# Retention, routed experts and an MLP in one kernel: buffers, the place of the bias and of the counts, and the order of loads at two seams

## The chip, the core and the metric

The kernel runs on one core of a Trainium2 chip as one launch. The metric is the device time of one execution in microseconds (us); the kernel before takes 1440.12 us in the median of three runs (1436.64 to 1443.65). In what follows PE is the matrix engine (PEld its weight loads), DVE, ACT and POOL are the vector, scalar and GpSimd engines, SP is the engine that issues most of the DMAs; SPq and ACTq are the queues of SP and ACT.

## The reference

Three steps, each on the output of the one before. Inputs are q, k, v of 8 sequences, 8 heads, 576 positions and 64 per head; then a mixture of 8 experts over 4608 tokens of 512 numbers; then an MLP of width 2048.

```python
# 1. retention: no softmax, a decay per head
gamma = 1.0 - 2.0 ** (-5.0 - np.arange(H))
Dmat = np.where(rel >= 0, gamma[:, None, None] ** rel, 0.0)       # rel = i - j
attn = np.matmul(q @ k.T / sqrt(64) * Dmat, v)
x = attn.transpose(0, 2, 1, 3).reshape(4608, 512)
# 2. each token goes to the expert with the largest logit
logits = x @ w_gate + modality_bias[modality_id]
e_idx = np.argmax(logits, axis=1)
gate_w = softmax(logits)[arange(N), e_idx]
out[mask] = gate_w[mask, None] * (relu(x[mask] @ w1[e]) @ w2[e])  # mask = e_idx == e
# 3.
h = out @ w_in
y = (h - tanh(h)) @ w_out
```

## The kernel before

**Retention, in tiles.** `for t in range(NTILE)` runs over 36 tiles of 128 tokens; nine tiles are two sequences. SP loads three arrays for a tile: qk, vk (`load_tile`) and, for the first nine, the decay factors gx (`load_gx`). They are loaded `AHEAD` = 4 tiles ahead. On PE a tile is the scores of the *next* tile (`scores(t+1)`, L305), and then `attend(t)`: the inter part, from the state of the tokens before (L341), the intra part, from the masked scores a and the scaled values vs (L349), and the update of the state (L364). DVE masks the scores (L309) and multiplies the result by gx into xt (L374). ACT copies the state (L368). POOL makes vs, the values times a decay, in `scaled` (L315), two tiles ahead and into two buffers. Inter comes ahead of intra, but for tiles without an inter part, the tile in which a sequence begins in its middle, and the last tile of all:

```python
after = not inter or mid_t or t == NTILE - 1
```

**Routing, in groups of four tiles.** `route_a`, `route_b` and `route_c` (L405 to L457) make logits, the expert of each token, its slot and its gate. The logits get `bias`, which five POOL operations make ahead of the loop from the modality ids (`mid`) and the two rows of bias (`mb`). `scatter` (L460, L461) has POOL write 128 token numbers into the list of their experts, slot_d, by an indirect DMA. `turn_x` turns a tile on PE (L472), `save_x` scales it by the gate on ACT into xo (L477; two buffers) and stores it to x_d (L478, on ACT's queue).

**The seam to the experts.** An expert's tokens are worked on in units of 400. `choose` (L380) counts after 28 of the 36 tiles and picks an expert that already has 400 tokens. Two tiles later SP loads their numbers (`load_ids`, L154) and POOL gathers the rows with four indirect DMAs (`gather_rows`, L158); PE turns them (`turn_rows`, L148), ACT and DVE split them into a high and a low part (xh L149, xl L150). So unit 0 begins while the routing of the last tiles is open; that is spread over its steps f = 0, 1, 2 (`rest_a`, `rest_b`, `rest_c`). `rest_c` turns the last four tiles on PE, counts (L567) and calls `table`, a chain of small DVE operations that writes which expert, slots and rows every further unit has (utab). `swap` then opens the buffers of the later stages, and issues those weight loads of unit 1 that had been put off (`pend`).

**Units.** A unit has 8 steps f, in each of which PE does 12 matmuls hp (L634) and 12 matmuls acc (L828 to L830); `load_raw` (L696) loads weights, `split_w` splits them on ACT (L703) and DVE (L704). `prep(u, f)` puts the work for the next unit into the steps: for unit 0 the ids of unit 1 at f = 2, their gather at f = 3, the turning of its four blocks of rows (`tr_x`) at f = 5, 6 and 7.

**MLP.** Nine blocks of 512 tokens, hp (L634) and acc (L902 to L904) again; its first matrix is kept in winh and winl, its second is prepared in DRAM during the units (wo_d).

The order on each engine is the order in which this code is written; a framework puts in the waits for buffers and data. A pool with n buffers of a name makes the (n+1)th user wait for the first to be done.

Of the kernel before, what the change touches and what calls it, by code (L numbers as in the profile page):

```python
# [21 lines left out]
DM = H * D  # L22
# [5 lines left out]
AHEAD = 4  # L28
# [73 lines left out]
def kernel(tc, A, out):  # L102
    nc = tc.nc
    with ExitStack() as ctx:
# [12 lines left out]
        wres = pool("wres", 1)  # L117

        ident = keep.tile([128, 128], F32, name="ident")
        winh = wres.tile([128, F3, DM], F32R, name="winh")  # L120
        winl = wres.tile([128, F3, DM], F32R, name="winl")

# [81 lines left out]
        with tc.manual_schedule():  # L204
# [9 lines left out]
            xo_p = p1r("xo", 2, side="right")  # L214
# [49 lines left out]
            load_gx(2)  # L264

# [46 lines left out]
            def scaled(t):  # L312
                qk, vk = gt[t]
                vs = tmp.tile([128, H, D], F32, name="vs")
# [7 lines left out]
            def attend(t):  # L322
# [7 lines left out]
                after = not inter or mid_t or t == NTILE - 1  # L330
# [149 lines left out]
            def store_x(t, spare=False):  # L480
# [7 lines left out]
            bt = xo_p.tile([128, DM], F32, name="xo")  # L488
            midf, midn = bt[:, 0:NTILE], bt[:, NTILE:2 * NTILE]
            b1 = bt[:, 2 * NTILE:(2 + E) * NTILE].rearrange("p (t e) -> p t e", e=E)  # L490
            nc.gpsimd.tensor_copy(out=midf, in_=mid[:, :, 0])
            nc.gpsimd.tensor_scalar(out=midn, in0=midf, scalar1=-1.0, scalar2=1.0, op0=ALU.mult, op1=ALU.add)
            sh = [128, NTILE, E]
            nc.gpsimd.tensor_tensor(out=bias, in0=midn.unsqueeze(2).to_broadcast(sh),
                                    in1=mb[:, 0:1, :].to_broadcast(sh), op=ALU.mult)
            nc.gpsimd.tensor_tensor(out=b1, in0=midf.unsqueeze(2).to_broadcast(sh),
                                    in1=mb[:, 1:2, :].to_broadcast(sh), op=ALU.mult)
            nc.gpsimd.tensor_tensor(out=bias, in0=bias, in1=b1, op=ALU.add)
# [5 lines left out]
            for t in range(NTILE):  # L504
# [5 lines left out]
                if t + 2 < NTILE:  # L510
                    scaled(t + 2)
                if t + AHEAD < NTILE:
                    load_tile(t + AHEAD)
                if t + 3 < PERIOD:
                    load_gx(t + 3)
# [47 lines left out]
            def rest_c():  # L563
                late.extend(range(g * RG, NTILE))
                late_x(RG)
                cp = ps_m.tile([128, E], F32, name="m")
                nc.tensor.matmul(out=cp, lhsT=ones, rhs=cum[:, NRG], start=True, stop=True)  # L567
                table(cp)

# [47 lines left out]
            c1.close()  # L617

# [45 lines left out]
            with ExitStack() as c2:  # L664
# [84 lines left out]
                def swap():  # L749
# [17 lines left out]
                    while pend:  # L767
                        load_raw(pend.pop(0))

                def prep(u, f):  # L770
# [10 lines left out]
                    if u + 1 < UMIN:  # L781
# [4 lines left out]
                        for s in {5: (0,), 6: (1, 2), 7: (3,)}.get(f, ()) if u == 0 else range(f - F1 + SE + 1, f - F1 + SE + 2):  # L786
                            if 0 <= s < SE:
                                tr_x(u + 1, s)
# [170 lines left out]
```

## Time and profile before

| | |
|---|---|
| median of three runs | 1440.12 us (1436.64 to 1443.65) |
| profiled execution | 1445.13 us, of which 1443.4 us are the span of the trace |
| PE busy | 1399.0 us, 97% |
| DVE, ACT, POOL busy | 1044.4, 683.5 and 221.1 us |

Times in the rows are counted from the span's start. Retention and routing fill the stretch up to some 160 us, unit 0 begins at 176 us, unit 1 at about 211, and the MLP fills the second half. In a row of a timeline, the bracket at the end is how long the engine stood idle just before and what ended that.

### The profile page before, as it was taken

To read this page: it belongs to the slowest core of one execution; us is meant where nothing else is said; L and a number is where in the kernel's file an instruction comes from. 1 tells how busy PE (TensorE), PEld (TensorE's weight loads), DVE (VectorE), ACT (ScalarE), POOL (GpSimd) and SP (SyncE) were. 2 spreads that over 40 slices of the span, in tenths; PEclk is the share of its full clock that TensorE was granted. 3 is DMA by queue.
4 is the path that set the end of the run, shared out by engine and by line. 5 is a ranking of instruction groups with operands and counts; after the bars stand their busy time and mean duration, and the time that the engine had idled before them with its cause. 6 is when DMAs were issued, how large, how long until landed. Compare 5 with 4: busy or idle time off the path is not lost.

```text
span 1443.4 us, 22522 instructions
## 1 busy us (share of the span) xinstructions
PE 1399.0 (97%) x8427; PEld 1215.6 (84%) x8427; DVE 1044.4 (72%) x1761; ACT 683.5 (47%) x1269; POOL 221.1 (15%) x288
## 2 busy tenths in 40 slices
PE   6999689999999999989999999999999999999997
PEld 5888589999999999977888888888888888888885
DVE  2666458888888888746777777777777777778764
ACT  0222244444444444444555555555555555565543
POOL 4455421111111111010111101111011110011101
PEclk8999889999999999999999999999999999999999
DMA  9999353454663345516000100001000000000000
GB/s 336 343 333 329 129 185 118 127 132 132 179 189 89 89 90 150 124 33 254 30 30 1 37 23 30 30 9 50 1 30 30 30 30 0 30 30 1 30 1 30
DMA packets 65682, 138.71 MB, mean 96 GB/s; under 512 B 22480, under 2 KB 29328, under 8 KB 65568
## 3 DMA queue, kind: packets, MB, share of 16 engines
q1 hardware_dynamic: 49360, 96.15, 22.1%
q0 software_dynamic: 7904, 21.96, 4.4%
q10 hardware_dynamic: 8304, 19.11, 3.5%
q8 instruction: 68, 1.11, 0.3%
q14 instruction: 46, 0.38, 0.1%
HBM read 135.16 MB, written 39.80 MB: 121 GB/s over the span
## 4 chain that ended last, share of the span: by engine, by line
PE 49%; issue 5%; POOL 0%; DMA 0%; DVE 0%; ACT 0%; POOLq 0%; DVEq 0%; ACTq 0%
PE hp L634 25%; PE acc L902 8%; PE acc L903 8%; PE acc L904 8%; POOL out_dram L927 0%; DMA wout<-wo_d 0%; DVE xh L878 0%; ACT xh L876 0%; DVE xl L885 0%; POOLq L955 0%; DVE xl L887 0%; DVE xl L877 0%; DVE xl L886 0%; POOL nopt L926 0%; DVE lo L881 0%
## 5 line engine op out<-in xcount | busy, mean ns | idle before, releaser
L875 ACT ACTIVATE xh<-hp 128x512 f32<-128x512 f32 x144 | 86.4, 600 | 331.7 <-PE hp L634 313.1
L902 PE MATMUL acc<-wout,hi 128*128 128x512 f32 x576 | 226.0, 392 | 5.2 <-DMA wout<-wo_d 5.2
L634 PE MATMUL hp<-yh,winh 128*128 128x512 f32 x576 | 226.4, 393 | 1.4 <-DVEq L849 1.4
L634 PE MATMUL hp<-yl,winh 128*128 128x512 f32 x576 | 226.2, 393 | 0.0
L634 PE MATMUL hp<-yh,winl 128*128 128x512 f32 x576 | 226.1, 393 | 0.0
L903 PE MATMUL acc<-wout,hi 128*128 128x512 f32 x576 | 225.9, 392 | 0.0
L904 PE MATMUL acc<-wout,lo 128*128 128x512 f32 x576 | 224.9, 390 | 0.0
L877 DVE TENSOR_TENSOR xl<-xh,hp 128x512 f32<-128x512 f32 x144 | 99.1, 688 | 167.8 <-ACT xh L876 167.8
L886 DVE SCALAR_TENSOR_TENSOR xl<-xh,xl 128x512 f32<-128x512 f32 x144 | 128.5, 893 | 15.4 <-DVE xl L885 0.5
L828 PE MATMUL acc<-hi,wh 128*128 128x400 f32 x384 | 137.9, 359 | 0.1
L902 PEld LDWEIGHTS acc<-wout,hi 128*128 128x128 f32 x576 | 108.7, 189 | 29.9 <-ACT xh L875 5.6
L634 PE MATMUL hp<-xl,wh 128*128 128x400 f32 x384 | 133.4, 348 | 0.4 <-DVE xl L150 0.4
L830 PE MATMUL acc<-hi,wl 128*128 128x400 f32 x384 | 133.4, 347 | 0.0
L634 PE MATMUL hp<-xh,wl 128*128 128x400 f32 x384 | 133.2, 347 | 0.0
L634 PE MATMUL hp<-xh,wh 128*128 128x400 f32 x384 | 133.0, 346 | 0.0
L829 PE MATMUL acc<-lo,wh 128*128 128x400 f32 x384 | 132.2, 344 | 0.0
L634 PEld LDWEIGHTS hp<-yh,winh 128*128 128x128 f32 x576 | 108.2, 188 | 25.7 <-PEq L849 1.7
L634 PEld LDWEIGHTS hp<-yh,winl 128*128 128x128 f32 x576 | 108.3, 188 | 24.7
L904 PEld LDWEIGHTS acc<-wout,lo 128*128 128x128 f32 x576 | 108.7, 189 | 23.9 <-DVE lo L881 0.4
L634 PEld LDWEIGHTS hp<-yl,winh 128*128 128x128 f32 x576 | 108.1, 188 | 23.9
L903 PEld LDWEIGHTS acc<-wout,hi 128*128 128x128 f32 x576 | 108.6, 188 | 23.2
L728 ACT ACTIVATE hi<-hp 128x400 fp32r<-128x400 f32 x96 | 48.5, 506 | 166.9 <-PE hp L634 166.9
(162 smaller groups left out, 2526.4 us busy)
## 6 DMA issues: line engine op xcount, KB each, us to landing
raw<-in_w_dram SPq DMA_DIRECT2D x91, 512.0 KB
qk<-in_qk_dram SPq DMA_DIRECT2D x36, 512.0 KB
vk<-in_vk_dram SPq DMA_DIRECT2D x35, 512.0 KB
y_d<-yo SPq DMA_DIRECT2D x12, 800.0 KB
yr<-y_d SPq DMA_DIRECT2D x9, 1024.0 KB
raw<-in_wo_dram SPq DMA_DIRECT2D x16, 512.0 KB
wo_d<-cv_em ACTq DMA_DIRECT2D x16, 512.0 KB
raw<-in_wi_dram SPq DMA_DIRECT2D x16, 512.0 KB
```

The source lines that it names most:

```text
L634: nc.tensor.matmul(out=hp, lhsT=lhs, rhs=rhs, start=j == 0, stop=j == 3 * KD - 1)
L728: nc.scalar.activation(out=hi, in_=hp, func=ACTF.Relu)
L828: nc.tensor.matmul(out=o, lhsT=wh[:, cs], rhs=hi, start=first, stop=False)
L829: nc.tensor.matmul(out=o, lhsT=wh[:, cs], rhs=lo, start=False, stop=False)
L830: nc.tensor.matmul(out=o, lhsT=wl[:, cs], rhs=hi, start=False, stop=last)
L875: nc.scalar.activation(out=u, in_=hp, func=ACTF.Square)
L877: nc.vector.tensor_tensor(out=v, in0=u, in1=hp, op=ALU.mult)
L886: nc.vector.scalar_tensor_tensor(out=v, in0=s, scalar=SQ_C, in1=v, op0=ALU.add, op1=ALU.mult)
L902: nc.tensor.matmul(out=acc[s], lhsT=hi, rhs=wh, start=first, stop=False)
L903: nc.tensor.matmul(out=acc[s], lhsT=hi, rhs=wl, start=False, stop=False)
L904: nc.tensor.matmul(out=acc[s], lhsT=lo, rhs=wh, start=False, stop=last)
```

## The change

Its edits:

- Loads run six tiles ahead (`AHEAD`), for gx as well; the loads of two more tiles stand ahead of the loop.
- vs has four buffers and is made four tiles ahead; xo has four buffers.
- The bias is made after tile 2 (`make_bias`) and not ahead of the loop.
- The last tile has inter ahead of intra, as most tiles have.
- In `rest_c` the count and `table` stand ahead of the last four turns.
- The room of winh and winl is taken when the first pools of the routing are closed, not from the start.
- The weight loads of unit 1 that had been put off are issued in `prep`, behind the ids of unit 1, and not in `swap`.
- Unit 1's blocks of rows are turned two in step 6 and two in step 7 of unit 0, in place of one, two and one in steps 5 to 7.

On POOL, the first vs products of the program and the bias (xo is the scratch tile of the bias), before:

```order
L315 TENSOR_TENSOR vs<-vk,vsc 128x512 x2
L491 CAST xo<-mid 128x36
L492 TENSOR_SCALAR xo<-xo 128x36
L494 TENSOR_TENSOR bias<-xo,mb 128x288
L496 TENSOR_TENSOR xo<-xo,mb 128x288
L498 TENSOR_TENSOR bias<-bias,xo 128x288
L315 TENSOR_TENSOR vs<-vk,vsc 128x512 x8
```

and after:

```order
L314 TENSOR_TENSOR vs<-vk,vsc 128x512 x7
L493 CAST xo<-mid 128x36
L494 TENSOR_SCALAR xo<-xo 128x36
L496 TENSOR_TENSOR bias<-xo,mb 128x288
L498 TENSOR_TENSOR xo<-xo,mb 128x288
L500 TENSOR_TENSOR bias<-bias,xo 128x288
L314 TENSOR_TENSOR vs<-vk,vsc 128x512 x5
```

Five further vs products stand ahead of the bias now: those of tiles 2 to 6.

On POOL, ahead of the gathers of unit 0's rows (L158 before, L154 after; nopt is a small memset that goes with each scatter), before:

```order
L460 MEMSET nopt 128x1
L461 DMA slot_d<-tokid,pos_s 37376x16
L460 MEMSET nopt 128x1
L461 DMA slot_d<-tokid,pos_s 37376x16
L315 TENSOR_TENSOR vs<-vk,vsc 128x512
L460 MEMSET nopt 128x1
L461 DMA slot_d<-tokid,pos_s 37376x16
L460 MEMSET nopt 128x1
L461 DMA slot_d<-tokid,pos_s 37376x16
L315 TENSOR_TENSOR vs<-vk,vsc 128x512
L158 DMA vk<-x_d,idt_74 128x512 x3
L158 DMA vk<-x_d,idt_74 16x512
```

and after:

```order
L314 TENSOR_TENSOR vs<-vk,vsc 128x512
L459 MEMSET nopt 128x1
L460 DMA slot_d<-tokid,pos_s 37376x16
L459 MEMSET nopt 128x1
L460 DMA slot_d<-tokid,pos_s 37376x16
L459 MEMSET nopt 128x1
L460 DMA slot_d<-tokid,pos_s 37376x16
L459 MEMSET nopt 128x1
L460 DMA slot_d<-tokid,pos_s 37376x16
L154 DMA vk<-x_d,idt_69 128x512 x3
L154 DMA vk<-x_d,idt_69 16x512
```

The vs products of the last two tiles stood between and behind the scatters; now the last vs of all is ahead of four scatters in a row.

On SP, behind the last row stores of the routing (x_d<-xg), where the loads for unit 1 begin (utab is the table of units, idt the ids, raw the weights), before:

```order
L679 TENSOR_LOAD utab
L679 ISA x2
L679 TENSOR_LOAD utab
L679 ISA x2
L696 ISA
L696 DMA raw_2516<-in_w_dram 128x1024
L696 ISA
L696 DMA raw_2518<-in_w_dram 128x1024
L679 TENSOR_LOAD utab
L679 ISA x2
L154 ISA
L154 DMA idt<-slot_d 128x4x1
```

and after:

```order
L687 TENSOR_LOAD utab
L687 ISA x2
L150 ISA
L150 DMA idt<-slot_d 128x4x1
L687 TENSOR_LOAD utab
L687 ISA x2
L687 TENSOR_LOAD utab
L687 ISA x2
L704 ISA
L704 DMA raw_2516<-in_w_dram 128x1024
L704 ISA
L704 DMA raw_2518<-in_w_dram 128x1024
```

The ids stood behind two weight loads; now they stand ahead of them.

```diff
--- before.py
+++ after.py
@@ -25,7 +25,7 @@
 TL = 128
 NTILE = NT // TL
 PERIOD = 9
-AHEAD = 4
+AHEAD = 6
 RG = 4
 NRG = NTILE // RG
 UE = 400
@@ -114,12 +114,8 @@
         tok_d = dram.tile([NT + UE, 1], I32, name="tok_d")
         wo_d = dram.tile([F3, 128, 2, DM], F32, name="wo_d")
         keep = pool("keep", 1)
-        wres = pool("wres", 1)
 
         ident = keep.tile([128, 128], F32, name="ident")
-        winh = wres.tile([128, F3, DM], F32R, name="winh")
-        winl = wres.tile([128, F3, DM], F32R, name="winl")
-
         xT_p = [pool("xTa", 1), None]
         idt0 = keep.tile([128, SE], I32, name="idt0")
         pick = keep.tile([1, 2], I32, name="pick")
@@ -211,7 +207,7 @@
             tmp = p1("tmp", 2)
             const = p1r("const", 1, side="right")
             xt_p = p1r("xt", 3, side="right")
-            xo_p = p1r("xo", 2, side="right")
+            xo_p = p1r("xo", 4, side="right")
             sm = p1r("sm", 2, side="right")
             ps_sc = p1("ps_sc", 3, space=PSUM)
             ps_x = p1("ps_x", 1, space=PSUM)
@@ -262,6 +258,9 @@
             nc.scalar.dma_start(out=mb.rearrange("p a e -> p (a e)"), in_=A["mb"].to_broadcast([128, 2 * E]))
             load_tile(3)
             load_gx(2)
+            for t in range(4, AHEAD):
+                load_tile(t)
+                load_gx(t - 1)
 
 
             nc.gpsimd.memset(ones, 1.0)
@@ -311,7 +310,7 @@
 
             def scaled(t):
                 qk, vk = gt[t]
-                vs = tmp.tile([128, H, D], F32, name="vs")
+                vs = tmp.tile([128, H, D], F32, name="vs", bufs=4)
                 nc.gpsimd.tensor_tensor(
                     out=vs, in0=vk[:, 0].rearrange("p (h d) -> p h d", h=H),
                     in1=vsc[:, t % PERIOD].unsqueeze(2).to_broadcast([128, H, D]), op=ALU.mult)
@@ -327,7 +326,7 @@
                 inter = r != 0
 
                 mid_t = r == PERIOD // 2
-                after = not inter or mid_t or t == NTILE - 1
+                after = not inter or mid_t
                 w = TL // 2 if mid_t else TL
 
                 def before():
@@ -485,17 +484,21 @@
             scaled(0)
             scores(0)
             scaled(1)
-            bt = xo_p.tile([128, DM], F32, name="xo")
-            midf, midn = bt[:, 0:NTILE], bt[:, NTILE:2 * NTILE]
-            b1 = bt[:, 2 * NTILE:(2 + E) * NTILE].rearrange("p (t e) -> p t e", e=E)
-            nc.gpsimd.tensor_copy(out=midf, in_=mid[:, :, 0])
-            nc.gpsimd.tensor_scalar(out=midn, in0=midf, scalar1=-1.0, scalar2=1.0, op0=ALU.mult, op1=ALU.add)
-            sh = [128, NTILE, E]
-            nc.gpsimd.tensor_tensor(out=bias, in0=midn.unsqueeze(2).to_broadcast(sh),
-                                    in1=mb[:, 0:1, :].to_broadcast(sh), op=ALU.mult)
-            nc.gpsimd.tensor_tensor(out=b1, in0=midf.unsqueeze(2).to_broadcast(sh),
-                                    in1=mb[:, 1:2, :].to_broadcast(sh), op=ALU.mult)
-            nc.gpsimd.tensor_tensor(out=bias, in0=bias, in1=b1, op=ALU.add)
+            scaled(2)
+            scaled(3)
+            def make_bias():
+                bt = xo_p.tile([128, DM], F32, name="xo")
+                midf, midn = bt[:, 0:NTILE], bt[:, NTILE:2 * NTILE]
+                b1 = bt[:, 2 * NTILE:(2 + E) * NTILE].rearrange("p (t e) -> p t e", e=E)
+                nc.gpsimd.tensor_copy(out=midf, in_=mid[:, :, 0])
+                nc.gpsimd.tensor_scalar(out=midn, in0=midf, scalar1=-1.0, scalar2=1.0, op0=ALU.mult, op1=ALU.add)
+                sh = [128, NTILE, E]
+                nc.gpsimd.tensor_tensor(out=bias, in0=midn.unsqueeze(2).to_broadcast(sh),
+                                        in1=mb[:, 0:1, :].to_broadcast(sh), op=ALU.mult)
+                nc.gpsimd.tensor_tensor(out=b1, in0=midf.unsqueeze(2).to_broadcast(sh),
+                                        in1=mb[:, 1:2, :].to_broadcast(sh), op=ALU.mult)
+                nc.gpsimd.tensor_tensor(out=bias, in0=bias, in1=b1, op=ALU.add)
+
             def due(w):
 
                 r = w - (EARLY - 1) * RG
@@ -507,12 +510,14 @@
                     scores(t + 1)
                 attend(t)
                 evac_x(t)
-                if t + 2 < NTILE:
-                    scaled(t + 2)
+                if t + 4 < NTILE:
+                    scaled(t + 4)
+                if t == 2:
+                    make_bias()
                 if t + AHEAD < NTILE:
                     load_tile(t + AHEAD)
-                if t + 3 < PERIOD:
-                    load_gx(t + 3)
+                if t + AHEAD - 1 < PERIOD:
+                    load_gx(t + AHEAD - 1)
                 if t >= RG + 3:
                     for w in due(t - RG - 3):
                         scatter(w)
@@ -561,11 +566,11 @@
                     scatter(g * RG + r)
 
             def rest_c():
-                late.extend(range(g * RG, NTILE))
-                late_x(RG)
                 cp = ps_m.tile([128, E], F32, name="m")
                 nc.tensor.matmul(out=cp, lhsT=ones, rhs=cum[:, NRG], start=True, stop=True)
                 table(cp)
+                late.extend(range(g * RG, NTILE))
+                late_x(RG)
 
 
             def table(cp):
@@ -615,6 +620,9 @@
             t_ahead = late.pop(0)
             tp_ahead = turn_x(t_ahead, False)
             c1.close()
+            wres = pool("wres", 1)
+            winh = wres.tile([128, F3, DM], F32R, name="winh")
+            winl = wres.tile([128, F3, DM], F32R, name="winl")
 
 
             def blocks(names, nf, lag, width, xT, load_w, gemm1_w, gemm2, post, prep, finish):
@@ -764,8 +772,6 @@
                         if f + 2 < len(cvs2):
                             fill2[-1] = lambda a=fill2[-1], b=cvs2[f + 2][0]: (a(), b())
                     fill2.reverse()
-                    while pend:
-                        load_raw(pend.pop(0))
 
                 def prep(u, f):
                     if u == "t":
@@ -783,9 +789,11 @@
                             idts[u + 1] = ids_of(u + 1)
                         if f == d + 1:
                             gather(u + 1, idts.pop(u + 1))
-                        for s in {5: (0,), 6: (1, 2), 7: (3,)}.get(f, ()) if u == 0 else range(f - F1 + SE + 1, f - F1 + SE + 2):
+                        for s in {6: (0, 1), 7: (2, 3)}.get(f, ()) if u == 0 else range(f - F1 + SE + 1, f - F1 + SE + 2):
                             if 0 <= s < SE:
                                 tr_x(u + 1, s)
+                    while pend and cvs2:
+                        load_raw(pend.pop(0))
                     if f == 3 and u - 1 in yos:
                         store(u - 1)
                         if (u - E + 1) * UE + E - 1 >= UB and yr0[0] is None:
```

## Rows read from the trace of the kernel before

**Rows 1.** Windows: stretch, length, busy time by engine, PE clock, DMA share, GB/s.

```profile
20.00:30.00 10.00, 5.66 (x64) 5.04 (x64) 1.78 (x3) 0.00 (x0) 4.54 (x7) 0.53 1.03 401
30.00:40.00 10.00, 10.00 (x186) 8.03 (x186) 5.30 (x9) 1.70 (x4) 3.13 (x3) 0.96 0.84 296
40.00:145.00 105.00, 105.00 (x1811) 86.31 (x1806) 72.23 (x185) 30.79 (x62) 52.17 (x75) 1.00 0.95 336
...
160.00:170.00 10.00, 3.24 (x47) 2.28 (x45) 1.82 (x9) 0.37 (x1) 7.77 (x13) 0.87 0.29 85
170.00:180.00 10.00, 8.29 (x32) 5.78 (x33) 4.08 (x7) 3.54 (x7) 0.00 (x0) 0.50 0.42 158
180.00:190.00 10.00, 9.87 (x67) 8.87 (x65) 7.27 (x24) 6.81 (x14) 2.11 (x3) 0.95 0.78 246
...
200.00:210.00 10.00, 6.51 (x29) 6.15 (x28) 4.51 (x9) 2.19 (x5) 3.77 (x4) 0.75 0.58 189
210.00:220.00 10.00, 10.00 (x56) 9.64 (x55) 5.55 (x10) 2.98 (x6) 0.00 (x0) 0.91 0.01 2
220.00:630.00 410.00, 409.56 (x2294) 401.41 (x2293) 322.21 (x578) 178.81 (x365) 44.94 (x44) 1.00 0.47 125
```

**Rows 2.** Timeline of the start: start, duration, engine, line, operation, tiles, idle before.

```profile
22.00 0.21 POOL L491 CAST xo<-mid 128x36 f32<-128x36 int32 x1 [10.99 <-DMA mid<-in_ids_dram]
...
26.38 2.04 POOL L315 TENSOR_TENSOR vs<-vk,vsc 128x512 f32<-128x512 f32 x2
...
27.48 1.98 PE L349 MATMUL xp<-a,vs 128*64 128x128 f32 x16 [2.79 <-POOL vs L315]
```

**Rows 3.** Timeline where the first expert is chosen.

```profile
147.52 0.96 POOL L461 DMA_INDIRECT slot_d<-tokid,pos_s  x1 [0.19 <-issue]
147.75 0.69 ACT L477 ACTIVATE xo<-m,gate 128x512 f32<-128x512 f32 x1 [2.06 <-DMA x_d<-xo]
...
148.48 0.17 PE L380 MATMUL m<-cum,ones 128*128 128x8 bf16 x1 [2.59 <-ACT xo L477]
```

**Rows 4.** Timeline of the seam between the last tiles and unit 0.

```profile
151.93 1.04 POOL L315 TENSOR_TENSOR vs<-vk,vsc 128x512 f32<-128x512 f32 x1 [3.44 <-PE st L364]
...
154.47 0.96 POOL L461 DMA_INDIRECT slot_d<-tokid,pos_s  x1 [0.19 <-issue]
...
156.68 0.42 SPq L154 DMA_DIRECT2D idt<-slot_d  x1
...
159.50 1.01 POOL L158 DMA_INDIRECT vk<-x_d,idt  x1 [2.12 <-issue]
...
161.51 0.67 PE L341 MATMUL xp<-qk,state 64*64 64x128 f32 x16
...
168.38 0.96 POOL L461 DMA_INDIRECT slot_d<-tokid,pos_s  x1 [0.19 <-issue]
...
170.96 0.69 DVE L374 TENSOR_TENSOR xt<-xp,gx 128x512 f32<-128x512 f32 x1 [7.72 <-remote]
...
171.68 1.44 SPq L696 DMA_DIRECT2D raw<-in_w_dram  x3
...
176.04 0.70 PE L634 MATMUL hp<-xh,wh 128*128 128x400 f32 x1
```

**Rows 5.** Timeline of unit 0's end, around the loads for unit 1.

```profile
189.83 0.15 DVE L585 COPY vals<-m 1x8 f32<-1x8 f32 x1
...
196.16 0.34 PE L634 MATMUL hp<-xh,wh 128*128 128x400 f32 x1
...
197.89 0.55 SPq L696 DMA_DIRECT2D raw<-in_w_dram  x2
...
199.65 0.39 SPq L154 DMA_DIRECT2D idt<-slot_d  x1
...
200.53 0.34 PE L634 MATMUL hp<-xh,wh 128*128 128x400 f32 x1
...
206.38 1.11 PE L148 MATMUL hp<-ident,xg 128*128 128x128 f32 x4 [3.49 <-DMA xg<-x_d,idt]
```

## The prediction

> **What bounds the kernel now.** I read the busy table first: PE is busy for 97% of the span, so only stretches in which it stands still, or runs at half clock, can give time back. The table of windows shows where these lie [rows 1]. From 220 to 630 us PE is busy for 409.56 of 410 us at clock 1.00. From 40 to 145 us, the loop over tiles, it is busy all the time too. PE's losses lie in three places: 20 to 30 us (5.66 busy of 10, clock 0.53), 160 to 180 us (3.24 and 8.29 busy, clock 0.87 and 0.50) and 200 to 210 us (6.51 busy, clock 0.75). All three lie ahead of a PE that is then full for 410 us, so a microsecond that PE gets back there should come off the end; nothing after 220 us is touched by the diff. Second I read the timeline of these places, for which wait ends last in each.
>
> At the start, PE's intra matmuls of tile 2 begin at 27.48, after 2.79 us of waiting for POOL's vs. POOL got to that product at 26.38 only, since the five bias operations, held by the load of the modality ids until 22.00, stand ahead of it in its order [rows 2].
>
> At the last tile, PE's L341 begins at 161.51 and is over at 162.18. DVE's product for it, which needs just that, starts at 170.96, with 7.72 us of idle time put down to "remote". Between lies POOL's run of eight indirect DMAs without a gap, four gathers from 159.50 and four scatters, the last from 168.38 to 169.34. The release comes 1.6 us after its end. Then raw weight loads (171.68), the routing's matmuls and the first expert matmul (176.04) follow, all behind that one release [rows 4]. What holds PE's signals for 8.8 us the trace doesn't say. It says when they are let go, and I tie the release to the end of POOL's run.
>
> At the second unit, PE waits 3.49 us for gathered rows (206.38). The gather's ids are loaded at 199.65, behind two weight loads on SP at 197.89 [rows 5].
>
> **The change part by part.**
>
> *Start: bias later, vs earlier.* POOL issues vs for tiles 0 to 6 ahead of the bias. Tile 2's vs then is ready long before 24.7, where PE starts to wait (27.48 - 2.79), and the whole wait of 2.8 us goes. Bias, five operations between 22.00 and 26.38, now stands behind seven products of 1.02 us each (2.04 for two); its first reader is the routing of the first four tiles, which PE comes to after tile 4, so I cost its move at nothing; were POOL late, DVE would wait there with PE's next masks behind it. Bounds: 0, if that tile's vk lands no sooner than 26.4, or if the DMA engines, at 1.03 in this stretch, bring the following tiles no sooner. Above: 2.8 plus what half clock cost after the wait. A clock of 0.53 in 20:30 and 0.96 in 30:40 leaves 0.8 us of half speed after 30, so 3.3 us from 27.48 on, half of it lost: 1.7, in all 4.5. I take 2.8, the row's own wait.
>
> *Prefetch of six tiles, four vs buffers.* PE is full from 40 to 145 us [rows 1], so there is nothing to shorten there. The DMA engines are busy for 0.95 of it, so they have 5 us to spare in 105; they must also bring the tiles 2.8 us sooner, which fits. A loss is possible: more loads in flight ahead of an outgoing row store can hold ACT. I cost it at 0, since PE stays a tile ahead of the routing, with a bound of one tile's time, 105/26 = 4.0 us.
>
> That six are in flight does not make the engines faster: the trace shows 336 GB/s at a share of 0.95 with four. The Trainium skill, "DMA: Bandwidth & Descriptors", section "Issuing engines are not separate DMA queues", says that DMAs from every issuing engine run on the same 16 DMA engines and interleave. By that rule the deeper prefetch competes with the first tiles' loads and with the x stores, the start's 2.8 us would be lost, and the sum would be 10.5, or 1429.6 us; the share of 1.03 there agrees with the rule, the slack after 30 us speaks against the loss.
>
> *Four outgoing-row buffers.* ACT's xo waits 2.06 us for an earlier store to let go of its buffer (147.75), and PE's count matmul for choosing the expert stands behind it for 2.59 us (148.48) [rows 3]. With four buffers the first wait goes, so PE may come 2.1 us sooner (0 to 2.6). It enters the sum only if POOL's run doesn't set the release.
>
> *The order on POOL before the gathers.* Before, scatters 24 and 25 are issued, the second at 147.52; then vs of tile 34 waits for PE until 151.93, then scatters 26 and 27 come, the last at 154.47; the ids are loaded at 156.68, 2.2 us after it [rows 3, 4]. After, all vs stand ahead, and the four scatters follow each other: at the 1.27 us of POOL's later run (159.50 to 168.38 for seven steps) the last comes at about 147.52 + 2 x 1.27 = 150.1, that is 4.4 us sooner, of which I count 4.3. The ids and the four gathers come as much sooner, and with the start's 2.8 us the run's end and the release come 7.1 us sooner. The scatters in the second half of the run need the routing of tiles 28 to 31, which comes sooner by the 2.8 and the 2.1 us above, so the run stays closed. Bounds: 2.2 less than 7.1, if it is that routing (2.1 sooner, not 4.3) which the run now waits for; 13.7 if no hold occurs (a rival below). Since the gathers gain more than PE, up to 1.8 us of the last tile's matmuls (L349 and L341) could fall behind the release; the 4.4 us from there to the first expert matmul (171.68 to 176.04) were the weights' arrival, whose buffers no longer wait for the last tile's xt, so I take 0 for it. Value 7.1, from 2.1 to 8.8 with the bounds of the start.
>
> *Last tile's order.* Intra after inter instead of before: the same 16 matmuls in the same place. 0 unless it is the cause of the hold.
>
> *Counts sooner.* DVE copies the counts at 189.83 without any idle time ahead of it [rows 5]; it is full there with weight splitting and routing, so counts from PE 2 us sooner would stand in its queue: 0. The four turns that now come behind them on PE hide as PE work that is only swapped: 0.
>
> *Second unit.* Ids go ahead of the two raw loads, so they start at about 197.9 and not 199.65: 1.8 us sooner, and rows land at about 204.6. The first turn moves from step 5 to 6. PE's step lasts 4.37 us (196.16 to 200.53) [rows 5]; PE reached the turn at 202.89 (206.38 - 3.49) and now reaches it at 207.3, 2.7 us after the rows. The second turn, now in the same step, wants rows that land 1.3 us after the first: also there. So the stall of 3.49 goes, and with it the half clock that followed: 5.0 us of it in 200:210 and 1.8 in 210:220 [rows 1], that is from 204.9 to about 211.8, in which PE worked 211.8 - 206.38 = 5.4 us, half of it lost: 2.7. Sum 6.2. Bounds: 3.0 (raw loads behind the ids, or turns packed into the last two steps ahead of unit 1's first matmul, cost PE a new wait of 3.2, nearly the old stall's size) to 6.9 (3.49 and half of all 6.8 us at low clock). I take 6.2.
>
> **Sum.** 7.1 + 6.2 = 13.3 us. The profiled execution took 1445.13 us, 1443.4 of span and 1.73 around it, 5 us over the median of 1440.12. Against itself it would come to 1431.8; taken off the median: 1426.8.
>
> **Rivals.**
> 1. *The hold vanishes.* It may come from something in PE's own order or from the late raw loads, not from POOL's run. For it: 8.8 us is out of proportion to anything PE had to do, and no other run of indirect DMAs in the timeline has a wait like it. Against: the release fits the run's end, and no other run is eight long. Then DVE gets the last tile at 162.2 - 2.8 - 2.1 = 157.3 in place of 170.96: 13.7; of the half clock (13.6 us in rows 160 to 190 [rows 1]) 2.5 more, with 4.6 as its limit; and 6.2: 22.4 in all, 1417.7 us.
> 2. *Only one half works.* Either the prefetch and POOL's earlier gathers bring nothing (the DMA share of 1.03 and the unmoved routing speak for it), leaving 6.2: 1433.9; or the second unit's rows or weights are late all the same, leaving 7.1: 1433.0. Against both: in each place a row names the instruction that stood ahead.
> 3. *More signals are held: slower.* The gathers move up by 4.3 us against 2.1 for PE, so the run begins while PE, DVE and ACT still pass tile 34 and 35 to each other (scores to mask, state to inter, xp to xt). In the rows one such signal was held for 8.8 us; if three more in series were held, 35.1 would stand where 8.8 stood: 26.3 less 13.3 slower, 1453 us. It decides from two more on (17.6 against 13.3). For it: one was held by just this run. Against: while the first two gathers ran, PE still came to L341 at 161.51, which needs ACT's copy of the state of the tile before [rows 4], so signals passed then; and a run of 10 us cannot hold three in series unless the scatters wait in between.
>
> **How the numbers follow.** The forecast has 0.45, the first rival 0.25, the second 0.23, the third 0.07. About 0.5% (7.2 us) is what a measurement of this kernel can tell from no change: faster is under 1432.9, slower over 1447.3. The forecast's own range is 1424.4 (all upper bounds, 15.7) to 1435.0 (all lower ones, 5.1); nearly all of it (0.43) and the first rival lie under 1432.9, of the second, whose two times stand close to that line, 0.08; 0.02 and 0.15 are within; the third is slower. So 0.76, 0.17, 0.07. The range for 8 in 10 takes in the first rival's time and the second's two, with 0.7 below and 3 above for their own bounds: 1417 to 1437.
>
> **What would show it.** Right: PE's intra of tile 2 with no wait for vs; four scatters in a row and the ids' load at about 149.5; the last tile's DVE product at about 164, 1.6 us after POOL's last scatter; no PE wait at unit 1's first turn and clock 1.00 from 200 to 220. Wrong: a DVE wait for the bias or a DMA wait of PE in the loop; the last tile's product well before POOL's run ends (rival 1) or several held signals (rival 3); a wait for raw weights at the second unit.

## The result and the profile after

The kernel after takes 1422.76 us in the median of four executions (1422.44 to 1423.35), the kernel before, timed beside it, 1438.38 us (1434.05 to 1443.65). The ratio is 0.989, with a 95% interval of 0.986 to 0.992: 15.6 us less by the medians, where 13.3 were forecast, and 1426.8 us as the time. After's executions lie within 1 us of each other, before's within 9.6. The profiled execution of after has a span of 1421.6 us, 21.8 less than the one of before; but that one, at 1445.13 us, was 6.75 us over this median, so the two traces show more than the change brings.

The windows of the kernel after, in the columns of [rows 1]:

```profile
20.00:30.00 10.00, 8.40 (x134) 7.41 (x136) 3.96 (x6) 0.62 (x2) 2.09 (x2) 0.83 1.02 400
...
40.00:145.00 105.00, 104.08 (x1782) 85.28 (x1777) 72.47 (x193) 31.99 (x64) 55.96 (x80) 1.00 0.93 342
...
160.00:170.00 10.00, 9.09 (x52) 8.01 (x53) 4.75 (x13) 3.91 (x10) 1.66 (x4) 0.83 0.40 145
170.00:180.00 10.00, 9.57 (x62) 9.28 (x60) 9.01 (x36) 5.76 (x11) 4.39 (x7) 1.00 0.92 328
...
200.00:210.00 10.00, 9.93 (x55) 9.59 (x54) 7.52 (x15) 3.81 (x9) 0.57 (x1) 1.00 0.31 105
...
220.00:630.00 410.00, 403.50 (x2245) 393.35 (x2245) 317.45 (x568) 178.78 (x361) 41.13 (x40) 1.00 0.47 122
```

Of the three stretches in which PE stood still, none is left as it was: 20 to 30 us has 8.40 us of PE work and not 5.66, 160 to 180 has 18.66 and not 11.53, 200 to 210 has 9.93 and not 6.51 at a clock of 1.00. PE's stretch of 410 us has 403.5 only because the pause ahead of the MLP, which ended after 630 us before, now lies partly inside it.

The timeline of the start, against [rows 2]:

```profile
22.55 1.97 PE L348 MATMUL xp<-a,vs 128*64 128x128 f32 x16
...
36.19 0.21 POOL L493 CAST xo<-mid 128x36 f32<-128x36 int32 x1
...
39.02 1.02 DVE L418 TENSOR_TENSOR lg<-lg,bias 128x32 f32<-128x32 f32 x1 [1.05 <-POOL bias L500]
```

PE's intra of tile 2 (22.55) waits for nothing, 4.9 us sooner than before. The bias begins at 36.19. DVE's first use of it waits 1.05 us (39.02).

The choice of the expert, against [rows 3], and the seam, against [rows 4]:

```profile
143.16 0.17 PE L379 MATMUL m<-cum,ones 128*128 128x8 bf16 x1 [0.42 <-ACT xo L476]
...
146.89 0.96 POOL L460 DMA_INDIRECT slot_d<-tokid,pos_s  x1 [0.19 <-issue]
...
149.11 0.42 SPq L150 DMA_DIRECT2D idt<-slot_d  x1
...
150.82 6.74 SPq L704 DMA_DIRECT2D raw<-in_w_dram  x3
...
151.93 0.99 POOL L154 DMA_INDIRECT vk<-x_d,idt  x1 [4.08 <-issue]
...
155.56 1.09 PE L348 MATMUL xp<-a,vs 128*64 128x128 f32 x16
...
156.71 0.69 DVE L373 TENSOR_TENSOR xt<-xp,gx 128x512 f32<-128x512 f32 x1 [0.55 <-PE xp L348]
...
160.37 0.39 PE L144 MATMUL xp<-ident,vk 16*128 16x16 f32 x4 [0.92 <-DMA vk<-x_d,idt]
...
160.78 0.96 POOL L460 DMA_INDIRECT slot_d<-tokid,pos_s  x1 [0.19 <-issue]
...
161.58 0.47 PE L642 MATMUL hp<-xh,wh 128*128 128x400 f32 x1 [0.23 <-ACT wh L711]
```

PE's count comes at 143.16 with 0.42 us of wait in place of 2.59. The last of the four scatters is at 146.89 (154.47 before), the ids' load at 149.11 (156.68), the first gather at 151.93 (159.50): 7.6 us each. DVE's product for the last tile comes at 156.71, right behind PE, in the middle of POOL's run of eight indirect DMAs, which is as closed as before and ends at 161.74. So the hold of 8.8 us has not moved to an earlier time; it isn't there. PE's last wait but a short one (0.23 us, for ACT) is for the fourth gather's rows (160.37), and the first expert matmul starts at 161.58 in place of 176.04.

The second unit, against [rows 5]:

```profile
174.98 0.15 DVE L590 COPY vals<-m 1x8 f32<-1x8 f32 x1
...
182.39 0.40 SPq L150 DMA_DIRECT2D idt<-slot_d  x1
...
184.33 0.95 SPq L704 DMA_DIRECT2D raw<-in_w_dram  x3
...
185.39 0.98 POOL L154 DMA_INDIRECT xg<-x_d,idt  x1 [7.57 <-DMA raw<-in_w_dram]
...
192.28 0.60 PE L144 MATMUL hp<-ident,xg 128*128 128x128 f32 x4
...
193.29 0.66 PE L144 MATMUL hp<-ident,xg 128*128 128x128 f32 x4 [0.41 <-DMA xg<-x_d,idt]
```

The ids are loaded ahead of the raw weights, PE's first turn waits for nothing and the second 0.41 us, in place of 3.49 and half clock behind it. DVE copies the counts (174.98) as one of its operations in a row, without idle time ahead of it.

### The profile page after: what moved, and what is told of

Read it like the earlier page. It is cut to its first block, busy times and chain, and to the rows that moved or that the text cites. A ratio compares the mean times of both kernels' runs of the same rounds, so it can differ in the third digit from the quotient of the medians.

```text
span 1421.6 us, 22507 instructions
## 1 busy us (share of the span) xinstructions
PE 1392.0 (98%) x8427; PEld 1210.5 (85%) x8427; DVE 1044.5 (73%) x1761; ACT 682.9 (48%) x1269; POOL 220.8 (16%) x288
## 4 chain that ended last, share of the span: by engine, by line
PE 50%; issue 5%; DVE 1%; POOL 0%; ACT 0%; POOLq 0%; DVEq 0%; ACTq 0%
PE hp L642 25%; PE acc L910 8%; PE acc L911 8%; PE acc L912 8%; POOL out_dram L935 0%; DVE xh L886 0%; DVE xl L893 0%; ACT xh L884 0%; DVE xl L895 0%; DVE xl L894 0%; DVE lo L889 0%; POOLq L963 0%; DVE xl L885 0%; POOL nopt L934 0%; ACT xh L883 0%
```

## The experiments

Each set of runs was on one chip, with the kernel before timed in turn with the others. Times are medians with the lowest and highest.

### First set: single parts put back or taken alone

Before in this set: 1443.6 us (1438.38 to 1449.95).

**last_old**: after, with the last tile's old order.

```diff
-                after = not inter or mid_t
+                after = not inter or mid_t or t == NTILE - 1
```

> The kernel after, with the last tile's intra part ahead of its inter part again, as before. In the trace after, the 8.8 us hold of PE's signals at the last tile is gone although POOL's run of eight indirect DMAs is as closed as before (151.93 to 161.74). Theory A: the last tile's order made the hold; then it comes back here, DVE's product for that tile starts 5 us or more after PE's last matmul of it, and the time is 1430 to 1436 us, with a spread of several us between executions as before has. Theory B: the hold hangs on where POOL's gathers and PE's last tiles stand to each other, or on SP's weight loads that waited for that product; then nothing moves: 1422 to 1424 us.

Measured: 1432.1 us (1431.31 to 1434.6), ratio to before 0.993 (0.990 to 0.995). The time is the one that theory A gave, but the trace has no long hold between the last tile and DVE: PE stands still earlier, beside POOL's runs, in gaps of up to 1.9 us. Without after beside it this decides nothing.

**last_new**: before, with the last tile's new order alone, the same line the other way.

> The kernel before, with only the last tile's order changed (inter ahead of intra). Theory A (the order made the hold): the hold goes, 1426 to 1430 us, with executions within 1 us of each other. Theory B (it did not): as before, 1434 to 1444 us with the same spread, and DVE's product for the last tile far behind PE.

Measured: 1445.7 us (1437.79 to 1448.34), ratio 0.999 (0.997 to 1.002). The order alone changes nothing that can be told, and its trace has a hold like before's:

```profile
165.48 1.09 PE L349 MATMUL xp<-a,vs 128*64 128x128 f32 x16
...
172.67 0.96 POOL L461 DMA_INDIRECT slot_d<-tokid,pos_s  x1 [0.19 <-issue]
...
174.46 0.69 DVE L374 TENSOR_TENSOR xt<-xp,gx 128x512 f32<-128x512 f32 x1 [6.94 <-remote]
```

PE is done with the last tile at 166.6, DVE's product comes at 174.46, 0.8 us after the end of POOL's run. Theory A, that the old order makes the hold, is refuted by this.

**unit_old**: after, with the second unit's edits undone.

```diff
-                        for s in {6: (0, 1), 7: (2, 3)}.get(f, ()) if u == 0 else ...
-                    while pend and cvs2:
-                        load_raw(pend.pop(0))
+                        for s in {5: (0,), 6: (1, 2), 7: (3,)}.get(f, ()) if u == 0 else ...
+                    while pend:                      # in swap() again
+                        load_raw(pend.pop(0))
```

> The kernel after, with the edits for the second unit undone (two weight loads ahead of the ids; turns in steps 5, 6 and 7). The forecast's term: 6.2 us more, 1429 us, with a PE wait of about 3.5 us for gathered rows and some 7 us of half clock behind it. Rival: the rows come in time anyway, since the routing ends earlier: 1423 us.

Measured: 1440.26 us (1435.13 to 1441.71), ratio 0.997 (0.995 to 0.999), 11 us more than expected. The trace shows why: up to 170 us the program is that of after, and yet PE is slow at the seam.

```profile
145.71 0.96 POOL L460 DMA_INDIRECT slot_d<-tokid,pos_s  x1 [0.19 <-issue]
...
146.61 0.29 PE L348 MATMUL xp<-a,vs 128*64 128x128 f32 x1 [0.43 <-issue]
...
146.97 0.96 POOL L460 DMA_INDIRECT slot_d<-tokid,pos_s  x1 [0.19 <-issue]
...
147.31 0.34 PE L363 MATMUL st<-vs,vk 128*64 128x64 f32 x3 [0.35 <-issue]
...
148.72 0.58 PE L363 MATMUL st<-vs,vk 128*64 128x64 f32 x12 [1.07 <-issue]
```

Between 146.2 and 148.7 PE gets through five matmuls in small pieces, while POOL issues scatters; it goes on 0.8 us after the last of them is over. "Issue" says that PE waited for nothing that the profile shows. After has no such gap in the same place. A little later there is a hold too: the state that PE has finished at 155.04 is copied by ACT at 158.48 only, 1.1 us after POOL's four gathers are over; last_old shows the same, from 155.68 to 158.84.

**buf_old**: after, with the start and the buffers as before.

```diff
-AHEAD = 6
+AHEAD = 4
-            xo_p = p1r("xo", 4, side="right")
+            xo_p = p1r("xo", 2, side="right")
-                vs = tmp.tile([128, H, D], F32, name="vs", bufs=4)
+                vs = tmp.tile([128, H, D], F32, name="vs")
-            scaled(2)
-            scaled(3)
+            make_bias()
-                if t + 4 < NTILE:
-                    scaled(t + 4)
-                if t == 2:
-                    make_bias()
+                if t + 2 < NTILE:
+                    scaled(t + 2)
```

> The kernel after, with the start and the buffers as before: four tiles ahead, two vs buffers made two tiles ahead, two xo buffers, bias ahead of the loop. The last tile's new order, the counts and the second unit stay. Theory A (the last tile's order made the hold): no hold, but the start's wait (2.8 to 3.2 us), the xo wait (2.1 us) and the later gathers come back: 1427 to 1430 us. Theory B (where POOL's vs products, scatters and gathers stand made it): the hold is back too, 1432 to 1440 us with a spread of several us.

Measured: 1440.58 us (1435.08 to 1443.59), ratio 0.998 (0.996 to 1.000). Its trace has the hold: POOL's run ends at 170.51, DVE's product comes at 172.12 after 7.72 us of idle time put down to "remote", just as in [rows 4], though the last tile has its new order. In this set every kernel made from after was slower than its edit can explain, so the set says little about sizes; that called for after itself as a control.

### Second set: with after as control

Before in this set: 1436.86 us (1434.96 to 1443.73), on the same chip as the first set.

**after_again**: after, unchanged.

> The kernel after, unchanged, as the control for the others of this call. Last time unit_old, which is the same program up to 170 us, had PE standing still in 145.9 to 148.7 and 157.2 to 158.9, inside POOL's runs of indirect DMAs, where after's trace had no such gap; so the hold isn't a matter of these programs' order alone. Theory C: the hold is PE's signals and PE's issue being slowed while POOL issues indirect DMAs back to back, and how much differs from one chip or execution to the next. Then this run shows such gaps too and takes 1426 to 1434 us where before takes 1440 or more. Theory D: it is in the program, and the second unit's edits somehow bring it; then after is again at 1422 to 1424 us without a gap.

Measured: 1423.31 us (1423.04 to 1423.83), ratio 0.990 (0.988 to 0.992), no gap of PE over 0.52 us between 145 and 162 us. 13.5 us less than before in this set.

**unit_old2**: unit_old again.

> The kernel after with the second unit's edits undone, again, now beside after on the same chip. The forecast's term: 6.2 us over after. Last time's trace had PE waiting 4.6 us for gathered rows and half clock in 200 to 210 us, which would make 6 to 8. If more than 10 us separate the two, the hold is in it too.

Measured: 1429.46 us (1427.13 to 1430.48), ratio 0.995 (0.993 to 0.996): 6.15 us over after, where the forecast's term was 6.2. The trace has the wait and the half clock behind it (0.83 in 190 to 200 us):

```profile
191.27 0.93 PE L144 MATMUL hp<-ident,xg 128*128 128x128 f32 x4 [3.70 <-DMA xg<-x_d,idt]
```

Against before in this set the same run is 7.4 us less: that is what the rest of the change brings without the second unit's edits, where the forecast had 7.1. The same program took 10.8 us longer in the first set; that the gaps at the seam come and go with something outside the program is shown by this pair.

**last_old2**: last_old again.

> The kernel after with the last tile's old order, again, beside after on the same chip. Theory A (the order makes the hold): 5 us or more over after, with a gap between PE's last matmul of the tile and DVE's product that after doesn't have. Theory C: within 1.5 us of after, with gaps of the same kind and size in both.

Measured: 1424.79 us (1423.83 to 1427.26), ratio 0.992 (0.989 to 0.994): 1.5 us over after, at the edge of what can be told here, and no hold:

```profile
156.35 0.67 PE L340 MATMUL xp<-qk,state 64*64 64x128 f32 x16
...
157.09 0.69 DVE L373 TENSOR_TENSOR xt<-xp,gx 128x512 f32<-128x512 f32 x1 [0.47 <-PE xp L340]
...
161.45 0.96 POOL L460 DMA_INDIRECT slot_d<-tokid,pos_s  x1 [0.19 <-issue]
```

**spaced**: after, with two memsets of 128x512 ahead of each scatter and each gather of unit 0.

```diff
-        nopt = keep.tile([128, 1], F32, name="nopt")
+        nopt = keep.tile([128, 512], F32, name="nopt")
             def scatter(t):
                 nc.gpsimd.memset(nopt, 0.0)
+                nc.gpsimd.memset(nopt, 0.0)
...
                     for s in range(SE):
+                        nc.gpsimd.memset(nopt, 0.0)
+                        nc.gpsimd.memset(nopt, 0.0)
                         gather_rows(s, idt0, x0[s], EARLY * RG * TL)
```

> The kernel after, with two memsets of 128x512 (0.52 us each) ahead of every scatter and of every gather of unit 0, so that POOL's indirect DMAs stand some 1.3 us apart instead of 0.3. Theory C (back-to-back indirect DMAs hold PE): PE's signals are let go in each gap, so no gap of PE over 1 us is left inside the runs; the run itself gets 4 us longer for each four, so that the time is within 5 us of after's on this chip to either side. If the hold has nothing to do with the spacing: the same gaps as in after, and the time 4 to 8 us more than after's on this chip.

Measured: 1422.63 us (1421.46 to 1423.36), ratio 0.990 (0.988 to 0.992): the same as after. As after had no hold in this set, nothing follows for the hold. The gathers came later as expected (a PE wait of 6.08 us, and the first expert matmul at 168.63 in place of 162.01), and those 6.6 us did not show in the time. They were given back in the MLP, which does nothing else than in after: its matmuls hp took 389 ns on average in place of 393.

### Third set: before again, and the addresses

Before in this set, on another chip: 1439.07 us (1431.14 to 1444.93).

**before_again**: before, unchanged, for a second trace.

> The kernel before, unchanged, for a second trace. In the trace of before PE's signals are held for 8.8 us at the last tile; in the last call's traces after, unit_old and last_old show no gap over 1 us there, in the call before that unit_old and last_old had gaps. Theory C (the hold comes and goes with the execution or the state of the chip, and before's median holds only part of it): before's executions again spread over 5 us or more, and the trace shows a hold between 0 and 9 us. Theory D (it is fixed in before's program): again 8 to 9 us.

Measured: 1438.8 us (1434.67 to 1443.82). The profiled execution took 1443.82 us, nearly what the first one took, and has no hold:

```profile
151.69 1.97 PE L349 MATMUL xp<-a,vs 128*64 128x128 f32 x16
...
154.62 1.04 POOL L315 TENSOR_TENSOR vs<-vk,vsc 128x512 f32<-128x512 f32 x1 [6.04 <-PE st L364]
...
159.37 0.42 SPq L154 DMA_DIRECT2D idt<-slot_d  x1
...
162.29 1.01 POOL L158 DMA_INDIRECT vk<-x_d,idt  x1 [2.22 <-issue]
...
164.21 0.67 PE L341 MATMUL xp<-qk,state 64*64 64x128 f32 x16
...
164.94 0.69 DVE L374 TENSOR_TENSOR xt<-xp,gx 128x512 f32<-128x512 f32 x1 [0.51 <-PE xp L341]
165.66 1.44 SPq L696 DMA_DIRECT2D raw<-in_w_dram  x3
...
166.12 0.86 POOL L158 DMA_INDIRECT vk<-x_d,idt  x1 [0.30 <-issue]
...
171.16 0.96 POOL L461 DMA_INDIRECT slot_d<-tokid,pos_s  x1 [0.19 <-issue]
...
172.34 0.57 PE L148 MATMUL xp<-ident,vk 16*128 16x16 f32 x4 [1.64 <-DMA vk<-x_d,idt]
...
173.74 0.70 PE L634 MATMUL hp<-xh,wh 128*128 128x400 f32 x1
```

DVE follows PE at once (164.94) in the midst of a closed run of eight. The semaphore events kept with the two traces agree: in before, PE's increments for the matmuls that end at 162.18, 163.48 and 165.01 stand at 170.94 to 171.06; here each follows its matmul within 0.05 us. The first expert matmul still starts at 173.74, only 2.3 us sooner than in the trace with the hold, because it waits for the fourth gather's rows (172.34). That gather was issued at 166.12 and took 6.2 us to arrive, beside three weight loads issued at 165.66, 166.22 and 166.76; in after it took 4.6 (155.74 to 160.37), with one of its three weight loads well ahead (150.82) and two behind it (156.70 and 157.23). And the gathers began at 162.29 and not at 159.50, since after the wait at the choice PE ran at half speed for a while (clock 0.77 in 145 to 160 us, and 1.00 in the first trace; its intra took 1.97 us and not 1.09), so that vs of tile 34 came at 154.62.

**before_spaced**: before, with the memsets of spaced.

> The kernel before, with two memsets of 128x512 ahead of every scatter and of every gather of unit 0, as in spaced. If back-to-back indirect DMAs make the hold, DVE's product for the last tile comes within 1 us of PE's last matmul of it, whatever before shows in this call, and executions spread by less than 3 us. If not, a hold like before's stands in it too. The gathers end later (PE waits for them some 6 us, as in spaced), and the larger scratch tile shifts what lies behind it in SBUF: in spaced the last 3420 matmuls took 783 us and not 791, so the time alone does not decide; 1425 to 1438 us.

Measured: 1437.18 us (1433.2 to 1439.7), ratio 1.000 (0.997 to 1.002). No hold in its trace, but none in that of before_again either, and the spread of 6.5 us is not under 3: inconclusive on what makes the hold. That spacing ends it is not shown. Its MLP's matmuls hp took 389 ns, those of before_again on the same chip 393.

**buf_old2**: buf_old again.

> The kernel after with the start and the buffers as before, again. The forecast's terms in it: the start 2.8, the gathers 4.3 sooner, so 7.1 us over after's 1423: 1430 us, when there is no hold. From the traces of before and after the start gave 3.2 and the choice of the expert 2.1. With a hold as in the first call: 1435 to 1443 us.

Measured: 1434.28 us (1430.77 to 1439.69), ratio 0.996 (0.994 to 0.999). No hold, and the gathers 7 us later than in after:

```profile
158.91 1.01 POOL L154 DMA_INDIRECT vk<-x_d,idt  x1 [2.51 <-issue]
...
161.31 0.69 DVE L373 TENSOR_TENSOR xt<-xp,gx 128x512 f32<-128x512 f32 x1 [0.55 <-PE xp L348]
...
168.15 0.66 PE L144 MATMUL sc<-ident,vk 128*128 128x128 f32 x4 [2.15 <-DMA vk<-x_d,idt]
...
170.11 0.47 PE L639 MATMUL hp<-xh,wh 128*128 128x400 f32 x1 [0.35 <-ACT wh L708]
```

The first expert matmul is at 170.11, 8.5 us after that of after. The median is 11 us over after's two medians, more than the forecast's 7.1, and the lowest execution 7.5 to 8; but after ran on another chip, so the size is rough. Beside before on its own chip it is 4.8 us less, which is what the second unit's edits bring without the start and the buffers, with those of the last tile and the counts (6.2 and 0 forecast; 4.8 has an interval of 2.2 to 8.9). Most of the spread that before has comes back with these edits undone (8.9 us, of 13.8 for before in this set).

**pad**: after, with the larger scratch tile and nothing else.

```diff
-        nopt = keep.tile([128, 1], F32, name="nopt")
+        nopt = keep.tile([128, 512], F32, name="nopt")
...
-                        nc.gpsimd.memset(nopt, 0.0)
+                        nc.gpsimd.memset(nopt[:, 0:1], 0.0)
```

> The kernel after with the scratch tile nopt of 128x512 instead of 128x1 numbers, of which the memsets still write one column: nothing is done differently, but all tiles allocated behind it lie 2044 bytes further on in each partition. In spaced, which has that tile too, the MLP's hp matmuls took 389 ns and not 393. If the addresses did that, this kernel has 389 ns and takes 1414 to 1416 us, less than before and after; if it was the later start or the spacing, it takes 1422 to 1424 us.

Measured: 1417.13 us (1415.89 to 1418.0), ratio to before 0.985 (0.981 to 0.989); 5.6 and 6.2 us less than after's two medians, which are of another chip, and the fastest kernel of this study. The groups of the MLP's matmuls from 650 us on, busy time and mean of one, of after:

```profile
L642 PE MATMUL hp<-yh,winh 128*128 128x512 f32 x547 | 214.8, 393 | 0.0
...
L911 PE MATMUL acc<-wout,hi 128*128 128x512 f32 x545 | 212.9, 391 | 0.0
```

and of pad:

```profile
L911 PE MATMUL acc<-wout,hi 128*128 128x512 f32 x555 | 216.0, 389 | 0.0
...
L642 PE MATMUL hp<-yh,winh 128*128 128x512 f32 x548 | 213.3, 389 | 0.0
```

393 against 389 ns: 4 ns for each of the MLP's 1728 matmuls hp are 6.9 us, about what the time shows. The same number of matmuls of the same shape read the same data; only the addresses of the tiles behind the scratch tile differ. The chip is not the cause: hp takes 393 ns in all eleven traces with the small tile and 389 in all three with the large one (spaced, before_spaced, pad), on both chips. The shift of 2044 bytes is no multiple of 8, so the alignment of the tiles may have changed as well as their place; the two were not tried apart.

## Why the prediction was right, and where it was not

**Right in the total.** 15.6 us in the first comparison and 13.5 in the second set, for 13.3 forecast; the measured 1422.76 lies 4 us under the forecast and inside the range. In the second set the two parts add up: 6.15 for the second unit and 7.4 for the rest.

**The second unit: right.** 6.2 forecast, 6.15 measured by undoing it alone (unit_old2 against after_again). The path was not quite as worked out: rows were to land 2.7 us ahead of the first turn, but the second turn waited 0.41 us, perhaps because POOL's gathers (from 185.39) shared the DMA engines with the raw loads issued at 184.33, which no run tried. The slack of a step was needed for this, not left over.

**The start: right, with a small miss.** 2.8 forecast. By PE's thousandth matmul, at some 75 us, after is 3.2 us ahead of before in the first two traces and 2.6 in the second two. The bias was costed at nothing, with the words that DVE would wait if POOL were late: it did, 1.05 us, because bias stands behind vs of tile 6, whose values have to be loaded first. It cost PE 0.40 us once, its wait for DVE's one-hot behind that in the loop.

**The prefetch: right.** From 40 to 145 us the DMA engines moved 342 GB/s at a share of 0.93, and 336 at 0.95 before. PE lost 0.9 us there (104.08 of 105), 0.42 of it the wait at the choice, which came into this stretch, and 0.40 the wait just named, and kept the start's gain. The Trainium skill ("DMA: Bandwidth & Descriptors", "Issuing engines are not separate DMA queues") has the DMAs of all issuing engines run on the same 16 DMA engines. The trace agrees: with six tiles in flight the engines moved hardly more than with four. The sum of 10.5 that was worked out by that rule did not come.

**The choice of the expert: right as a wait.** The 2.59 us went to 0.42. Its time was not missing from the sum: vs of tile 34 waited for PE behind this wait, so the 4.3 us of the scatters hold it already. In before_again the same wait was followed by half clock, which made the gathers 2.8 us later. That is a part of before's spread that the first trace, with its clock of 1.00 there, didn't show.

**The gathers: right.** 7.1 us sooner forecast, 7.6 measured: 3.2 from the start (PE's lead at 75 us) and 4.4 by the four scatters in a row.

**The release: wrong.** The step that failed is "I tie the release to the end of POOL's run". In three traces it fits: the held product comes 1.6, 0.8 and 1.6 us after the run's end in before, last_new and buf_old. But runs of eight as closed as this stand in after and in before_again too, and there nothing is held. The hold comes and goes, in one and the same program. Where nothing is held, what bounds the first expert matmul is the arrival of the last gathered rows: 160.37 in after, 172.34 in before_again, each followed by the matmul 1.2 to 1.4 us later. A gather that starts sooner frees the expert sooner by as much, with or without the hold, so the term could be right in size for a wrong reason, which is luck: by medians it is 7.4 (unit_old2) to 11 (buf_old2). The traces of before, both of executions longer than the median, show more, 14.5 and 12.2 us at the first expert matmul; without the hold, 7.6 of the 12.2 are the start of the gathers, 2.8 the half clock in before_again, and 1.6 come of the fourth gather, which took 4.6 us to land in place of 6.2. The last of these was not counted, and what makes it was not tried.

**The rivals.** The first, that the hold vanishes, is what the two first traces show (21.8 us of span, 22.4 in the rival), but not what the change brings in the median. The two traces of before are of executions of 1445.13 us with the hold and 1443.82 without it, both 5 us or more over their medians: without the hold before is hardly faster, since the rows come late, and in how many executions of before it stands no run shows. Of the two causes that it named, the last tile's order is refuted by last_new, which has the order and the hold; the raw loads were not tried alone. The second and third did not come about.

**Open.** What makes PE's signals late beside POOL's indirect DMAs in some executions and not in others. It did not hang on the last tile's order (last_new). The five traces that have it, or gaps of over 1 us at the seam, are the first one of before and all four of the first set; a second trace of before, last_old, unit_old and buf_old, of another set, has no product held, and after's two traces have none. That these runs cause it is argued from where the gaps lie; spacing them out met no hold to remove. Before's spread is another matter: its executions go with the clock that was granted to them. In the third set they run from 1431.14 us at a mean clock of 0.993 to 1444.93 at 0.984. As an estimate, the missing share of the clock times the span is 10 us for the one and 23 for the other, so nearly the whole spread of 13.8 us. After's executions have 0.993 to 0.995. A longer pause and the half clock behind it come together, so this does not tell what begins it. Also not tried: the counts' edit by itself, whose zero rests on DVE's row alone (174.98).

## What to carry to other kernels

Follow a late start back over every hand (scatter, ids, gather, landing) and move the earliest of them that waits for something it doesn't need; here a product for a later tile stood between two scatters. Where a trace shows one long wait of unknown cause, take a second trace of the same program before building a term on it. Where executions of one program differ, compare their granted clocks first: here a pause cost its own length and, in some executions, the half clock behind it. And compare the mean time of the longest group of equal matmuls between variants: a shift of addresses may be worth as much as an edit.

## What the runs showed of the chip that was not expected

- PE's finished work was signalled up to 8.8 us late while POOL issued indirect DMAs, in some executions (before); in others of the same program at once (before_again). That POOL's DMAs cause it is not shown.
- With a tile of 2 KB more per partition ahead of the others in SBUF, the MLP's 128x512 matmuls hp took 389 ns in place of 393 in the mean, with pad some 6 us in 1420. Why these addresses are better, the runs don't tell.
- One program took 1440.26 and 1429.46 us in two sets on the same chip, a difference larger than most edits here. Only kernels of one set can be compared closely.
